# Earlier filler matmuls in any free bank, another order of loads, and the last output in three parts, in a fused RetNet and MLP kernel

## The chip, the cores and the metric

The kernel runs on one core of a Trainium2 chip. The metric is the device time of one execution in microseconds (us), the median over several runs. A core has a matrix engine (TensorE, "PE" in the profile), three engines for elementwise work (VectorE "DVE", ScalarE "ACT", GpSimd "POOL"), a queue engine that mostly issues transfers (SyncE, "SP"), and 16 DMA engines that move data between HBM and on-chip memory. Matrix products land in PSUM, which has eight banks; the other on-chip memory is SBUF.

## What is computed

The first half is a linear-attention recurrence over 4 batches, 8 heads, 768 positions and a head size of 64. Its output, 3072 tokens of 512 numbers, goes through a two-layer network with a squared ReLU.

```python
gamma = 1.0 - 2.0 ** (-5.0 - np.arange(H))
for t in range(S):
    state = gamma * state + einsum('bhd,bhe->bhde', k[:, :, t], v[:, :, t])
    y[:, :, t] = scale * einsum('bhd,bhde->bhe', q[:, :, t], state)
x = y.transpose(0, 2, 1, 3).reshape(3072, 512)
h = maximum(x @ w_in, 0)          # w_in: 512 x 2048
out = (h * h) @ w_out             # w_out: 2048 x 512
```

Inputs and output are float32; the matrix products run on bfloat16 copies.

## The kernel before, in words

**Tiling.** The 3072 tokens are cut into 24 chunks of 128. The recurrence is done chunk by chunk: inside a chunk through a masked score matrix, between chunks through a 64 x 64 state for each head. Chunks 0 and 1, and chunks 2 and 3, are handled as pairs ("pair 0" and "pair 2" below) by the functions `together` and `pair_visits`; a pair's q, k and v are loaded by one DMA each of 512 KB (L418). From chunk 4 on every chunk has its own loads of 256 KB (L588) and a "visit" on TensorE. The keys and queries are cast to bfloat16, transposed (by TensorE with an identity matrix for the early chunks, L447 and L641, by a DMA transpose for most later ones, L632) and multiplied.

**The two layers.** Chunks are gathered in blocks (`BLOCKS`, of 1, 2 or 4 chunks). `ffn1` makes the hidden layer of a block in groups, each filling one PSUM bank (matmuls on L807, ReLU on ScalarE on L812, the square on VectorE on L817). For a block of two chunks a group is 8 matmuls of 256 columns and covers 2 of the 16 slices of the hidden layer, so a block has 8 groups. `ffn2` makes the output of one chunk from 16 matmuls of 512 columns in one bank (L851), in four steps of four, one step for each piece of w_out; ScalarE copies the bank out (L859), SyncE stores it (L863). For the last chunk the output is made in two halves of 256 columns, one after the other.

**Weights.** w_in comes in six pieces: `i0` to `i3` of 512 KB each (halves of the first two quarters), `i4` and `i5` of 1 MB. w_out comes in four pieces `o0` to `o3` of 1 MB. Each lands as float32 in one of four staging buffers (`wst`) and is cast to bfloat16 in two to four steps by whichever of VectorE, ScalarE and GpSimd the plan picks (L401, L399, L403). All these loads are issued by SyncE in one queue.

**The order of the work.** Every step is an entry of a plan (`Plan.add`), with an engine or several to choose from, an expected duration, what it reads and writes, and a priority. `Plan.schedule` walks through planned time and takes always the step that can start first, ties by priority; the resulting order is fixed in the program, engine by engine. `HOME` binds single steps to an engine, `RANK` overrides a priority, `ORDER` gives the order of the first loads (letter and number: q, k, v of a chunk, `i` and `o` a piece of weights). `PACE` is the chunk from which a visit's priority competes with the two layers. Four PSUM banks (`fps`, NBANK = 4) are shared by transposes, sums and both layers; `sc` and `yy` hold the scores and outputs of the recurrence.

**Fillers.** In a span of planned time that ends at `WARM` + 1 and starts at `WARM - WARMING`, the plan counts for every TensorE step the time that TensorE would idle before it and puts in so many matmuls of 256 columns on the identity matrix (L905), each planned at `FILL` = 0.215 us. Nothing reads what they write. Before the change this span is 14.5 to 21 us, the fillers write to the last of the four banks, and that bank is kept from all other steps until 21 us.

Of the kernel before, what the change touches and what calls it, by code (L numbers as in the profile page):

```python
# [14 lines left out]
AF = mybir.ActivationFunctionType  # L15
# [3 lines left out]
class Plan:  # L19
# [48 lines left out]
    def schedule(self, nbanks, max_open):  # L68
# [17 lines left out]
                    pool[e].add(o["i"])  # L86
        if "PE" in eng_free:
            eng_free["PE"] = 0.06 * PRE
        bank_free = [0.0] * (nbanks - 1) + [WARM + 1]
        bank_of = {}  # L90
        open_groups = set()
        closed = {}
# [5 lines left out]
        while done < n:  # L98
# [25 lines left out]
            if move:  # L124
# [4 lines left out]
                while sum(x[1] for x in out_) + n_desc > self.RING:  # L129
                    t = max(t, out_.pop(0)[0])  # L130
            start[i] = t
            b = o["bank"]
            if b is not None and b[0] == "open":
                k = min((x, j) for j, x in enumerate(bank_free) if x is not None)[1]
# [4 lines left out]
            if move:  # L139
                eng_free[eng] = t + hold  # L140
                if n_desc:
                    made = max(made, t + self.GEN_LATENCY) + gen
                    ready = made + 0.15
                else:
                    ready = t + hold + 0.5
                pipe = max(max(pipe, t + self.DMA_LATENCY) + cost, ready)
                late = [y for y in (max(max(y, t + self.DMA_LATENCY) + cost, ready) for y in late) if y > pipe + 0.05]
                end[i] = max([pipe] + late) + self.LAND
                out_.append((max([pipe] + late), n_desc))
                dur = hold  # L150
            else:
                if eng == "PE":
                    o["fill"] = 0
                    if WARM - WARMING < t < WARM + 1:
                        o["fill"] = int(max(0.0, t - max(eng_free[eng], WARM - WARMING) - 0.1) / FILL)
                    issued += 2 * o["fill"]
                    before = issued
                    todo, per = 2 * o["count"], dur / max(1, 2 * o["count"])
                    now = t
                    while issued + todo > edge:  # L160
                        step = max(0, edge - issued)
                        now = max(now + step * per, next_fetched)
                        issued, todo = max(issued, edge), todo - step
                        ahead = next((y for x, y in reversed(history) if x <= edge - self.AHEAD), 0.0)
                        ahead = max(ahead, crossed)
                        crossed = now
                        edge += self.BLOCK
                        next_fetched = ahead + min(5.7, max(0.3, pipe - ahead)) + self.FETCH
                    issued += todo
                    dur = now + todo * per - t  # L170
                    history.append((issued, t + dur))
                    if any(before < x <= issued for x in range(self.BLOCK0 - self.AHEAD, issued + 1, self.BLOCK)):
                        late.append(max(pipe, t + 0.4) + 1.27)
                    o["dur"] = dur
                eng_free[eng] = t + dur
                end[i] = t + dur + o["lat"]
# [26 lines left out]
AHEAD = 4  # L203
WARM = 20.0
FILL = 0.215
WARMING = 5.5
PACE = 8
LEAD = 2
NPE = 7
NTD = 8  # L210
PRE = 0
WHALF = 2
WHALFD = (0.60, 1.47, 33, 0.6)
CVT = {'DVE': 0.69, 'POOL': 1.1}
TCAST = {'DVE': 0.43, 'ACT': 0.63, 'POOL': 0.78}
TEVAC = {'ACT': 0.6, 'DVE': 0.62}
NPAIR = 2
F2LAG = 3.0
F2WAIT = 4
CAST = {"k": {"DVE": 0.43, "ACT": 0.63, "POOL": 0.78}, "q": {"DVE": 0.43, "ACT": 0.63, "POOL": 0.78}}  # L220
WCAST = {"DVE": 0.43, "ACT": 0.63, "POOL": 0.78}
EVAC = {"ACT": 0.6, "DVE": 0.62}
WPRIO = {"in": -2.0, "out": 2.0}


HOME = {'ck5': 'ACT', 'cq5': 'ACT', 'Eq0.0': 'DVE', 'cv0.0': 'DVE', 'ck0.0': 'DVE', 'cwin5.2': 'DVE', 'cv2.1': 'POOL', 'ck2.0': 'DVE', 'cwin5.0': 'DVE', 'cwin2.0': 'POOL', 'cwout0.3': 'POOL', 'cwin1.0': 'POOL', 'ck0.1': 'DVE', 'ck2.1': 'DVE'}
RANK = {}
ORDER = (
    "q0 k0 o0 i0 v0 q2 k2 o1 v2 i1 v4 i2 k4 i3 i4 q4 i5 k5 v5 v6 o2 o3 q5 v7 k6 q6 k7 q7"
)  # L230


# [8 lines left out]
def kernel(  # L241
# [279 lines left out]
    def pair_visits(m):  # L521
# [3 lines left out]
        for b2 in range(2):  # L525
            pl.add(f"A{m}.{b2}", "PE", 0.4, [f"qkT{q0}.{x}.{b2}" for x in "kq"] + [f"qkT{q0 + c}.{x}" for c in range(2) for x in "kq"],
                   banks[b2], lambda b2=b2: pair_scores(m, b2), prio=-300 + m, lat=0.25, count=16)
            for a in range(2):
                pl.add(f"P{m}.{b2}{a}", "DVE", 0.68, (banks[b2][a], "cmask2"), (f"ptp{w}.{b2}{a}",),
                       lambda b2=b2, a=a: nc.vector.tensor_tensor(  # L530
                           out=pts2[w][:, b2, a], in0=held_by[b2][:, a, :].rearrange("s (g j t) -> s g j t", g=2, j=2),
                           in1=cmask2[:, :, None, :].to_broadcast([P, 2, 2, C]), op=ALU.mult),
                       prio=urgency(m))
        tw = [f"twin{x}{w}.{b2}" for x in "kv" for b2 in range(2)]
        for c in range(2):
            if c == 1 and i + 1 == NCH - 1:
                continue
            o1 = {}
            i0 = pl.add(f"B{m + c}", "PE", 0.3, tw, (f"gB{m + c}",),
                        lambda c=c, o1=o1: pair_sums(m, c, fps[o1["op"]["bank_index"]]), prio=-290 + m, lat=0.25,  # L540
                        count=16, bank=("open", ("B", m + c), False))
            o1["op"] = pl.ops[i0]
            twin_users.append(i0)
            j0, j1 = state(m + c, 0), state(m + c + 1, 0)
            first = i + c == 0

            def add_up(j0=j0, j1=j1, first=first, o1=o1):
                cc = fps[o1["op"]["bank_index"]][:, 0:256].rearrange("s (p t) -> s p t", p=NJ)
                if first:
                    nc.vector.tensor_copy(sts[j1][:], cc)  # L550
                else:
                    nc.vector.tensor_tensor(out=sts[j1][:], in0=cc, in1=sts[j0][:], op=ALU.add)
            pl.add(f"S{m + c}", "DVE", 0.42, (f"gB{m + c}",) if first else (f"gB{m + c}", f"S{j0}"), (f"S{j1}",), add_up,
                   prio=urgency(m) - 0.5, bank=("close", ("B", m + c)))
        for b2 in range(2):
            def values_and_state(b2=b2):
# [272 lines left out]
    def rows(m):  # L829
        return where(m)[0] * S + where(m)[1] * C  # L830

    def ffn2(blk):
        for q4 in range(blk0[blk], blk0[blk] + blocks[blk]):
            g, u = divmod(q4, 4)
            h2 = h2s[g % NH2]
            slot = q4 % NOSB
            parts = 2 if q4 == NM - 1 else 1
            w = DM // parts
            for part in range(parts):
                ns = slice(part * w, part * w + w)  # L840
                grp = ("f2", q4, part)
                keys = [f"osb{slot}.{part}"] if parts > 1 else [f"osb{slot}.0", f"osb{slot}.1"]
                o1 = {}
                for j in range(4):
                    reads = [f"h{g % NH2}.{u}.{4 * j + c}" for c in range(4)] + [f"wout{j}.{c}.{h}" for c in range(4) for h in range(2)]

                    def mm(j=j, o1=o1, h2=h2, u=u, ns=ns, w=w):
                        ps = fps[o1["op"]["bank_index"]]
                        for c in range(4):
                            fb = 4 * j + c  # L850
                            nc.tensor.matmul(ps[:, 0:w], lhsT=h2[:, fb, u * C : u * C + C], rhs=w_out_bf[j][:, c, ns],  # L851
                                             start=(fb == 0), stop=(fb == NFB - 1))
                    i0 = pl.add(f"F2.{q4}.{j}" + f"/{part}" * (parts > 1), "PE", 0.866 / parts, reads, (f"g{grp}",), mm,
                                prio=(q4 + F2LAG) * 8 + 2 * j + 1 + part * 9, lat=0.2,
                                bank=("open", grp, True) if j == 0 else ("use", grp), count=4)
                    if j == 0:
                        o1["op"] = pl.ops[i0]
                pl.add(f"O{q4}" + f"/{part}" * (parts > 1), "ACT", 0.2 + 0.4 / parts, (f"g{grp}",), keys,
                       lambda o1=o1, slot=slot, ns=ns, w=w: nc.scalar.activation(  # L859
                           osbs[slot][:, ns], fps[o1["op"]["bank_index"]][:, 0:w], AF.Copy),  # L860
                       prio=q4, bank=("close", grp))
                pl.add(f"st{q4}" + f"/{part}" * (parts > 1), "SP", STORE, keys, (),
                       lambda q4=q4, slot=slot, ns=ns: nc.sync.dma_start(out[rows(q4) : rows(q4) + C, ns], osbs[slot][:, ns]),  # L863
                       prio=-1)

    dma_prio = {x: n for n, x in enumerate(dma_order(NM))}
# [30 lines left out]
    if tc is not None:  # L897
        with tc.manual_schedule():
# [3 lines left out]
            for i in sequence:  # L902
                o = pl.ops[i]
                for _ in range(o.get("fill", 0)):
                    nc.tensor.matmul(fps[NBANK - 1][:, 0 : 2 * P], lhsT=ident[:],  # L905
                                     rhs=ident[:, None, :].to_broadcast([P, 2, P]), start=True, stop=True)
                o["fn"](o["on"]) if o["flex"] else o["fn"]()
    return pl
# [30 lines left out]
```

## Time and profile before

| what | us |
|---|---|
| median of 6 runs | 213.9 (212.88 to 214.45) |
| the profiled execution | 214.32 |
| its span in the profile | 212.6 |
| TensorE busy with matmuls | 195.7 |
| first layer's matmuls (L807), busy | 92.7 |
| second layer's matmuls (L851), busy | 89.7 |
| first matmul of any kind starts | 5.41 |
| first matmul of the first layer starts | 17.70 |
| last copy of the output ends (209.36 + 0.38) | 209.74 |

The page cuts the span in 40 slices and prints the busy tenths of each engine, so one slice is 5.3 us. "Waits" name an engine and line, what it waited for, the total in us, how often, and the longest. In the timeline a row is start, duration, engine, line, operation, output<-inputs, shapes and count; in square brackets stands how long the engine idled before, and who ended that. Matmuls of a row overlap each other, so a row's duration is from the first start to the last end.

### The profile page before, as it was taken

The page shows a single profiled execution, that of the slowest core. Times are in us where ns is not written, and L with a number is a line of the kernel's source. Part 1 is how long each engine was busy: PE and PEld are TensorE (multiplying, and loading weights), DVE is VectorE, ACT ScalarE, POOL GpSimd, SP SyncE. Part 2 cuts the span into 40 slices and gives each one's busy share as a digit, 9 for nine tenths or more (in the row PEclk, how much of TensorE's full clock was granted, in tenths as well). Part 3 has the DMA queues.
Part 4 walks back from the last instruction along what each step waited for, and adds up shares of the span by engine and source line. Part 5 has one row for each costly group of instructions (what it writes and reads, how often), then busy time and mean ns, then how long its engine had stood idle before and what let it go on. Part 6 is the DMA issues. An engine that isn't in the chain of part 4 may idle for free.

```text
span 212.6 us, 5916 instructions
## 1 busy us (share of the span) xinstructions
PE 195.7 (92%) x2545; PEld 116.9 (55%) x2570; DVE 115.0 (54%) x253; ACT 88.4 (42%) x148; POOL 42.0 (20%) x69
## 2 busy tenths in 40 slices
PE   0689799998999899999999999999999999999993
PEld 0457596773676757766654444454444444444453
DVE  3687879747385866367570765846463442322100
ACT  8335376653342434433322365223534324534221
POOL 6345333124322121312221232022000000000000
PEclk9999999999999999999999999999999999999999
DMA  6999999999899999999989997999111011011022
GB/s 164 307 301 264 328 375 315 256 310 217 226 200 179 213 208 238 241 173 200 257 176 239 246 243 146 176 228 219 25 52 52 0 52 49 0 49 51 3 99 99
DMA packets 94442, 38.13 MB, mean 179 GB/s; under 512 B 79952, under 2 KB 88400, under 8 KB 94416
## 3 DMA queue, kind: packets, MB, share of 16 engines
q1 hardware_dynamic: 94416, 37.76, 80.7%
q8 instruction: 20, 0.33, 0.7%
q14 instruction: 6, 0.05, 0.1%
HBM read 27.26 MB, written 6.29 MB: 158 GB/s over the span
## 4 chain that ended last, share of the span: by engine, by line
PE 62%; DMA 21%; SPq 11%; issue 1%; ACT 1%; DVE 1%; POOL 1%; ACTq 0%; POOLq 0%
PE fps L851 32%; PE fps L807 25%; DMA qn<-in_q_dram 7%; DMA wst<-in_moe_w_out_dram 5%; DMA kn<-in_k_dram 4%; SPq L781 4%; SPq L418 4%; DMA qkT<-kqs 3%; SPq L588 2%; DMA vn<-in_v_dram 2%; PE yy L658 2%; PE yy L673 1%; PE sc L684 1%; SPq L632 1%; PE sc L695 1%
## 5 line engine op out<-in xcount | busy, mean ns | idle before, releaser
L807 PE MATMUL fps<-xt,w_in 128*128 128x256 bf16 (+2 forms) x637 | 92.7, 294 | 1.3 <-POOL w_in L403 1.1
L851 PE MATMUL fps<-w_out,h 128*128 128x512 bf16 (+1 forms) x378 | 89.7, 370 | 2.4 <-POOL w_out L403 0.8
L812 ACT ACTIVATE h<-fps 128x512 bf16<-128x512 f32 x96 | 56.9, 596 | 76.4 <-PE fps L807 76.0
L807 PEld LDWEIGHTS <-w_in 128*128 128x128 bf16 x640 | 56.9, 98 | 32.0 <-POOL w_in L403 1.4
L817 DVE TENSOR_TENSOR h<-h 128x512 bf16<-128x512 bf16 x96 | 43.0, 458 | 48.9 <-ACT h L812 48.5
L851 PEld LDWEIGHTS <-h 128*128 128x128 bf16 x400 | 37.7, 98 | 37.5 <-issue 0.8
L859 ACT ACTIVATE osb<-fps 128x512 f32<-128x512 f32 (+1 forms) x25 | 14.5, 580 | 31.8 <-PE fps L851 31.5
L403 POOL CAST kqs<-kn 128x512 bf16<-128x512 f32 x19 | 12.6, 664 | 54.7 <-DMA kn<-in_k_dram 35.9
L760 DVE TENSOR_TENSOR xt<-yy,yf 128x512 bf16<-128x512 f32 x20 | 13.7, 686 | 16.2 <-PE yy L673 12.0
L403 POOL CAST kqs<-qn 128x512 bf16<-128x512 f32 x19 | 12.5, 656 | 19.9 <-DMA qn<-in_q_dram 18.2
L599 DVE TENSOR_TENSOR vs<-vn,vf 128x512 bf16<-128x512 f32 x20 | 13.6, 684 | 4.0 <-DMA vn<-in_v_dram 4.0
L751 DVE TENSOR_TENSOR state<-sc,state 128x256 bf16<-128x256 f32 x33 | 13.8, 419 | 0.5
L738 DVE TENSOR_TENSOR pt<-sc,cmask 128x512 bf16<-128x512 f32 x20 | 13.6, 680 | 0.0
L447 PE MATMUL fps<-ident,h 128*128 128x128 bf16 x32 | 4.6, 309 | 6.1 <-DVE h L401 6.1
L673 PE MATMUL yy<-qkT,state 64*64 64x64 bf16 x296 | 10.0, 197 | 0.2
L658 PEld LDWEIGHTS <-vs 64*64 64x64 bf16 x320 | 4.2, 107 | 6.9 <-issue 6.8
L684 PE MATMUL sc<-qkT 64*64 64x64 bf16 x320 | 6.2, 194 | 0.9 <-DMA qkT<-kqs 0.9
L399 ACT ACTIVATE qkT<-fps 128x512 bf16<-128x512 bf16 x8 | 4.7, 596 | 5.3 <-PE fps L447 4.7
L447 PEld LDWEIGHTS <-h 128*128 128x128 bf16 x32 | 3.0, 135 | 7.0 <-DVE h L401 6.4
L403 POOL CAST w_out<-wst 128x512 bf16<-128x512 f32 x5 | 4.0, 806 | 13.2 <-DMA wst<-in_moe_w_out_dram 13.2
L403 POOL CAST w_in<-wst 128x512 bf16<-128x512 f32 x6 | 4.7, 784 | 9.3 <-DMA wst<-in_moe_w_in_dram 9.3
L658 PE MATMUL yy<-pt,vs 64*64 64x64 bf16 x320 | 6.4, 198 | 0.1
(65 smaller groups left out, 88.5 us busy)
## 6 DMA issues: line engine op xcount, KB each, us to landing
out_dram<-osb SPq DMA_DIRECT2D x23, 256.0 KB, 3.8
vn<-in_v_dram SPq DMA_DIRECT2D x20, 256.0 KB, 5.0
kn<-in_k_dram SPq DMA_DIRECT2D x20, 256.0 KB, 4.9
qn<-in_q_dram SPq DMA_DIRECT2D x20, 256.0 KB, 4.7
wst<-in_moe_w_out_dram SPq DMA_DIRECT2D x4, 1024.0 KB, 9.7
wst<-in_moe_w_in_dram SPq DMA_DIRECT2D x4, 512.0 KB, 7.7
wst<-in_moe_w_in_dram SPq DMA_DIRECT2D x2, 1024.0 KB, 9.4
qn<-in_q_dram SPq DMA_DIRECT2D x2, 512.0 KB, 6.0
```

The lines of the kernel that those rows point to most:

```text
L403: nc.gpsimd.tensor_copy(o, t)
L599: lambda: nc.vector.tensor_tensor(out=o[:], in0=t.rearrange("s (h d) -> s h d", h=H), in1=vf[:, i, :, None].to_broadcast([P, H, D]), op=AL ...
L658: nc.tensor.matmul(yy[L * c : L * c + L, sub, p * L : p * L + L], lhsT=vs[r, 4 * a + j, :], rhs=pt[r, a, j, :], start=(p == 0), stop=True, ...
L673: nc.tensor.matmul(yy[L * c : L * c + L, sub, p * L : p * L + L], lhsT=st[r, j, :], rhs=qkT[r, 1, j, sub * L : sub * L + L], start=False, ...
L738: lambda: nc.vector.tensor_tensor(out=pt[:], in0=sc[:, :, 0:256].rearrange("s g (p t) -> s g p t", p=NJ), in1=cmask[:, None, None, :].to_b ...
L751: f = lambda cc=cc, j1=j1, j0=j0: nc.vector.tensor_tensor(out=sts[j1][:], in0=cc, in1=sts[j0][:], op=ALU.add)
L760: lambda: nc.vector.tensor_tensor(out=xt[:, :, u * C : u * C + C].rearrange("s p (g t) -> s g p t", g=2), in0=yy[:, :, 0:256].rearrange("s ...
L807: nc.tensor.matmul(ps[:, u * n : u * n + n], lhsT=w_in_bf[j][:, cb, c * P : (c + 1) * P], rhs=xt[:, cb, cols], start=(cb == 0), stop=(cb = ...
L812: nc.scalar.activation(h2[:, f0 : f0 + per, cols], ps[:].rearrange("p (u n) -> p u n", u=per), AF.Relu)
L817: nc.vector.tensor_mul(hv, hv, hv)
L851: nc.tensor.matmul(ps[:, 0:w], lhsT=h2[:, fb, u * C : u * C + C], rhs=w_out_bf[j][:, c, ns], start=(fb == 0), stop=(fb == NFB - 1))
L859: lambda o1=o1, slot=slot, ns=ns, w=w: nc.scalar.activation(osbs[slot][:, ns], fps[o1["op"]["bank_index"]][:, 0:w], AF.Copy),
```

## The change

The span in which fillers may be placed now starts at 1.6 us of planned time (`WARMING` 18.4) instead of 14.5. No bank is kept back for them: a filler goes to the bank that has been free longest, if there is one free at the time at which TensorE falls idle. The order of loads is new: both pairs' q, k and v and chunk 4's k come first, then w_in with chunk 4's v in between, then the first half of w_out. `PACE` goes from 8 to 6, the planned cost of GpSimd's scaling of v from 1.1 to 1.3 us, `HOME` has other entries, one of the four decay tables (`yf2`) gets a later priority, and the copy of a batch's first state may go to ScalarE. The output of the last chunk is made in three parts of 256, 128 and 128 columns, and the store of the last part is issued by ScalarE instead of SyncE. A branch for steps named in `ROUND` is added; `ROUND` is empty.

```diff
-        bank_free = [0.0] * (nbanks - 1) + [WARM + 1]
+        bank_free = [0.0] * nbanks
...
+            before_open = list(bank_free)
...
-                    if WARM - WARMING < t < WARM + 1:
+                    free = [(x, j) for j, x in enumerate(before_open) if x is not None and x <= max(eng_free[eng], WARM - WARMING)]
+                    if WARM - WARMING < t < WARM + 1 and free:
                         o["fill"] = int(max(0.0, t - max(eng_free[eng], WARM - WARMING) - 0.1) / FILL)
+                        o["fill_bank"] = min(free)[1]
...
-WARMING = 5.5
-PACE = 8
+WARMING = 18.4
+PACE = 6
...
-CVT = {'DVE': 0.69, 'POOL': 1.1}
+CVT = {'DVE': 0.69, 'POOL': 1.3}
...
+LAST = [256, 128, 128]
...
-HOME = {'ck5': 'ACT', 'cq5': 'ACT', 'Eq0.0': 'DVE', 'cv0.0': 'DVE', 'ck0.0': 'DVE', 'cwin5.2': 'DVE', 'cv2.1': 'POOL', 'ck2.0': 'DVE', 'cwin5.0': 'DVE', 'cwin2.0': 'POOL', 'cwout0.3': 'POOL', 'cwin1.0': 'POOL', 'ck0.1': 'DVE', 'ck2.1': 'DVE'}
-RANK = {}
+HOME = {'cwin5.0': 'DVE', 'cv0.1': 'DVE', 'cwin3.0': 'ACT', 'cq0.0': 'DVE', 'cwin1.0': 'DVE', 'cwin4.2': 'DVE', 'ck4': 'ACT', 'cwin5.3': 'ACT', 'cwin0.0': 'ACT', 'cwin5.1': 'ACT', 'cv0.0': 'DVE', 'cwin4.0': 'DVE', 'cq2.0': 'ACT'}
+ROUND = []
+RANK = {'yf2': -1.9}
 ORDER = (
-    "q0 k0 o0 i0 v0 q2 k2 o1 v2 i1 v4 i2 k4 i3 i4 q4 i5 k5 v5 v6 o2 o3 q5 v7 k6 q6 k7 q7"
+    "k0 q0 v0 k2 k4 q2 v2 i0 i1 i2 i3 i4 v4 i5 q4 v5 o0 o1 q5 k5 o2 k6 o3 k7 q6 v6 q7 v7"
 )
...
-            def add_up(j0=j0, j1=j1, first=first, o1=o1):
+            def add_up(on="DVE", j0=j0, j1=j1, first=first, o1=o1):
                 cc = fps[o1["op"]["bank_index"]][:, 0:256].rearrange("s (p t) -> s p t", p=NJ)
                 if first:
-                    nc.vector.tensor_copy(sts[j1][:], cc)
+                    copy_on(on, sts[j1][:], cc)
...
-            parts = 2 if q4 == NM - 1 else 1
-            w = DM // parts
-            for part in range(parts):
-                ns = slice(part * w, part * w + w)
+            widths = LAST if q4 == NM - 1 else [DM]
+            parts = len(widths)
+            for part, w in enumerate(widths):
+                lo = sum(widths[:part])
+                ns = slice(lo, lo + w)
...
-                pl.add(f"st{q4}" + f"/{part}" * (parts > 1), "SP", STORE, keys, (),
-                       lambda q4=q4, slot=slot, ns=ns: nc.sync.dma_start(out[rows(q4) : rows(q4) + C, ns], osbs[slot][:, ns]),
+                at_end = parts > 1 and part == parts - 1
+                pl.add(f"st{q4}" + f"/{part}" * (parts > 1), "ACT" if at_end else "SP", STORE, keys, (),
+                       lambda q4=q4, slot=slot, ns=ns, at_end=at_end: (nc.scalar if at_end else nc.sync).dma_start(
+                           out[rows(q4) : rows(q4) + C, ns], osbs[slot][:, ns]),
                        prio=-1)
...
-                    nc.tensor.matmul(fps[NBANK - 1][:, 0 : 2 * P], lhsT=ident[:],
+                    nc.tensor.matmul(fps[o["fill_bank"]][:, 0 : 2 * P], lhsT=ident[:],
                                      rhs=ident[:, None, :].to_broadcast([P, 2, P]), start=True, stop=True)
```

The plan's durations for the last chunk's steps follow the widths of the parts.

More of the change, by code (lines that the diff above doesn't have):

```diff
@@ L528, in pair_visits @@
             for a in range(2):
+                if f"P{m}.{b2}{a}" in ROUND:
+                    t = pts2[w][:, b2, a]
+                    pl.add(f"Pc{m}.{b2}{a}", "ACT", 0.6, (banks[b2][a],), (f"ptp{w}.{b2}{a}",),
+                           lambda b2=b2, a=a, t=t: nc.scalar.activation(
+                               t, held_by[b2][:, a, :].rearrange("s (g j t) -> s g j t", g=2, j=2), AF.Copy), prio=urgency(m))
+                    pl.add(f"Pm{m}.{b2}{a}", "POOL", 1.2, (f"ptp{w}.{b2}{a}", "cmask2"), (f"ptp{w}.{b2}{a}",),
+                           lambda t=t: nc.gpsimd.tensor_tensor(
+                               out=t, in0=t, in1=cmask2[:, :, None, :].to_broadcast([P, 2, 2, C]), op=ALU.mult),
+                           prio=urgency(m))
+                    continue
                 pl.add(f"P{m}.{b2}{a}", "DVE", 0.68, (banks[b2][a], "cmask2"), (f"ptp{w}.{b2}{a}",),
@@ L545, in pair_visits @@
             first = i + c == 0
-            def add_up(j0=j0, j1=j1, first=first, o1=o1):
+            def add_up(on="DVE", j0=j0, j1=j1, first=first, o1=o1):
                 cc = fps[o1["op"]["bank_index"]][:, 0:256].rearrange("s (p t) -> s p t", p=NJ)
                 if first:
-                    nc.vector.tensor_copy(sts[j1][:], cc)
+                    copy_on(on, sts[j1][:], cc)
                 else:
                     nc.vector.tensor_tensor(out=sts[j1][:], in0=cc, in1=sts[j0][:], op=ALU.add)
-            pl.add(f"S{m + c}", "DVE", 0.42, (f"gB{m + c}",) if first else (f"gB{m + c}", f"S{j0}"), (f"S{j1}",), add_up,
+            pl.add(f"S{m + c}", {"DVE": 0.42, "ACT": 0.45} if first else "DVE", 0.42, (f"gB{m + c}",) if first else (f"gB{m + c}", f"S{j0}"), (f"S{j1}",), add_up,
                    prio=urgency(m) - 0.5, bank=("close", ("B", m + c)))
@@ L836, in ffn2 @@
             slot = q4 % NOSB
-            parts = 2 if q4 == NM - 1 else 1
-            w = DM // parts
-            for part in range(parts):
-                ns = slice(part * w, part * w + w)
+            widths = LAST if q4 == NM - 1 else [DM]
[3 more added lines that the diff above has]
+                ns = slice(lo, lo + w)
                 grp = ("f2", q4, part)
-                keys = [f"osb{slot}.{part}"] if parts > 1 else [f"osb{slot}.0", f"osb{slot}.1"]
+                keys = [f"osb{slot}.{part}"] if parts > 1 else [f"osb{slot}.{y}" for y in range(len(LAST))]
                 o1 = {}
@@ L852, in mm @@
                                              start=(fb == 0), stop=(fb == NFB - 1))
[L853 removed]
+                    i0 = pl.add(f"F2.{q4}.{j}" + f"/{part}" * (parts > 1), "PE", 0.866 * w / DM, reads, (f"g{grp}",), mm,
                                 prio=(q4 + F2LAG) * 8 + 2 * j + 1 + part * 9, lat=0.2,
@@ L857, in ffn2 @@
                         o1["op"] = pl.ops[i0]
-                pl.add(f"O{q4}" + f"/{part}" * (parts > 1), "ACT", 0.2 + 0.4 / parts, (f"g{grp}",), keys,
+                pl.add(f"O{q4}" + f"/{part}" * (parts > 1), "ACT", 0.2 + 0.4 * w / DM, (f"g{grp}",), keys,
                        lambda o1=o1, slot=slot, ns=ns, w=w: nc.scalar.activation(
```

## The prediction

> **What bounds the kernel now.** I read the page first (busy shares, slices), then the waits of TensorE, then the timeline of the first 26 us, then the chain of waits at the end.
>
> ```profile
> span 212.6 us, 5916 instructions
> PE 195.7 (92%) x2545; PEld 116.9 (55%) x2570; DVE 115.0 (54%) x253; ACT 88.4 (42%) x148; POOL 42.0 (20%) x69
> PE   0689799998999899999999999999999999999993
> DMA  6999999999899999999989997999111011011022
> ```
>
> See two things: TensorE is full from about slice 5 on, and the DMA engines are full until slice 28, 150 us. So the end is "the moment at which TensorE has work without gaps, plus the work that is left". The gaps, from TensorE's waits:
>
> ```profile
> PE fps L447 <- DVE h L401: 6.1, 2, 5.4
> PE fps L494 <- DVE h L434: 1.2, 1, 1.2
> PE fps L807 <- POOL w_in L403: 1.1, 1, 1.1
> PE sc L684 <- DMA qkT<-kqs: 0.9, 2, 0.6
> PE fps L851 <- POOL w_out L403: 0.8, 1, 0.8
> ```
>
> After 26 us only 0.8 (at 48.5 us, for the last piece of w_out) and 0.9 are left. What the change can win lies in the first 26 us:
>
> ```profile
> 12.55 0.60 PE L447 MATMUL fps<-ident,h 128*128 128x128 bf16 x4
> 16.14 0.63 PE L905 MATMUL fps<-ident 128*128 128x256 bf16 x2
> 17.13 0.64 PE L478 MATMUL sc<-qkT 64*64 64x128 bf16 x16
> 17.70 1.35 PE L807 MATMUL fps<-xt,w_in 128*128 128x256 bf16 x8
> 18.99 0.42 PE L478 MATMUL yy<-qkT 64*64 64x128 bf16 x16
> 19.74 1.04 PE L807 MATMUL fps<-xt,w_in 128*128 128x256 bf16 x8
> 22.38 1.05 PE L807 MATMUL fps<-xt,w_in 128*128 128x256 bf16 x8
> 23.49 1.23 PE L807 MATMUL fps<-xt,w_in 128*128 128x256 bf16 x8
> 25.84 1.38 PE L807 MATMUL fps<-xt,w_in 128*128 128x256 bf16 x11 [1.12 <-POOL w_in L403]
> ```
>
> The same 16 score matmuls take 0.64 us before 18.4 us and 0.42 after: the array is at half rate until then (the trace's clock record turns to 1.0 at 18.37; the slice row prints 9 all along and does not show it). By 25.84 us four groups of the first layer are done; a group of 8 at 256 columns takes 0.87 us at full rate (the chain of waits has "0.87 PE fps L807 x8"). What held them is w_in:
>
> ```profile
> 20.00 0.63 ACT L399 ACTIVATE w_in<-wst 128x512 bf16<-128x512 f32 x1 [0.30 <-DMA wst<-in_moe_w_in_dram]
> 24.88 0.43 DVE L401 CAST w_in<-wst 128x512 bf16<-128x512 f32 x1 [0.81 <-DMA wst<-in_moe_w_in_dram]
> ```
>
> The trace's landing records give spacings of full streaming: 1.80 us per 512 KB pair load, 1.50 per half piece of weights (512 KB), 2.75 per 1 MB piece, 1.04 per 256 KB load. Streaming alone would put the fourth half piece (i3) at 22.0; it landed at 24.86. Fifteen DMA engines finished i2 by 18.45, the last at 19.98. The records of queue q8 show a 16 KB packet starting at 17.01, another at 22.35; each time the slowest engine falls back, by 1.5 and 1.3 us, and that lag of 2.85 stays through 42 us.
>
> The end:
>
> ```profile
> 207.66 0.38 ACT L859 ACTIVATE osb<-fps 128x256 f32<-128x256 f32 x1 [1.15 <-PE fps L851]
> 209.36 0.38 ACT L859 ACTIVATE osb<-fps 128x256 f32<-128x256 f32 x1 [1.31 <-PE fps L851]
> ```
>
> **What the skill says.** (1) "TensorE: Matmul & The Clock Gate", Part 1: the array starts at half clock and gets full clock after about 3.4 us of sustained activity, judged in free-running windows. The trace agrees: TensorE is busy without long gaps from 11.8 us, and the clock rises at 18.37. (2) "Runtime: NRT & Kernel Launch", Instruction fetch mechanics: instructions come in 16 KiB blocks of 256 by a DMA of the sequencer, a cost that is mostly hidden. The blocks agree (2545+2570 TensorE instructions / 256 = 20; q8 has 20 packets; 17.01 and 22.35 lie at about instruction 276 and 532), but hidden it is not: the 1.5 us above. (3) "DMA: Bandwidth & Descriptors", Issuing engines are not separate DMA queues: another issuing engine saves only sequencer time. No trace here has a store from ScalarE.
>
> **The change, part by part.**
>
> *Fillers.* They may now start from 1.6 us of the plan and use any free bank. Until the first transpose at about 5.4 us that is (5.4-1.6-0.1)/0.215 = 17 fillers, 34 instructions; perhaps 12 more in later gaps. They run where TensorE waits for data; a filler is 256 columns, 0.11 us warm (0.87/8), twice that cold, planned as 0.215, so it fits its gap. Cost on the path: 0, covered by those waits; if data comes earlier than planned, one gap's fillers, up to 0.3. A filler that waits for its bank's reader delays only the step behind it, which waits for data too. Gain: full clock by about 5.1 to 8.5 instead of 18.4. On pair 0 and pair 2 each burst gets 0.2 shorter, some six on a pair's chain, 1.2 us. This is not summed: the loads bound those pairs. It is needed, because TensorE now would idle until w_in comes.
>
> *Loads.* Streaming spacings from the first landing at 4.9: k0 4.9, q0 6.7, v0 8.5, k2 10.3, k4 11.35, q2 13.15, v2 14.95, then i0 16.45, i1 17.95, i2 19.45, i3 20.95, i4 23.7, v4 24.7, i5 27.5, q4 28.5, v5 29.5, o0 32.3, o1 35.0, q5 36.1, k5 37.1, o2 39.9, k6 40.9, o3 43.7. Instruction fetches come on top. Pair 0 has 240 TensorE instructions (16 transposes, 32 scores, 32 sums, 32 values, 8 applies, times two), with fillers the 276th falls at about 11 us, and the 532nd at the end of pair 2, about 18. I take the same 1.5 and 1.3 us: v2 16.45, i0 17.95, i1 20.8, i2 22.3, i3 23.8, i4 26.5, i5 30.3, o3 46.6. Between landing and use lie casts, 0.75 to 0.98 (i3 before: 24.86 to 25.84); I take 0.85. HOME moves casts between engines, PACE and RANK shift ties; these engines are 20 to 54% busy, and I price them at 0, with 0.3 either way.
>
> *TensorE from there.* xt of pair 0 is ready at about 13, of pair 2 at about 19. Each half piece now feeds two groups, 1.74 us. i0: 18.8 to 20.6. i1: usable 21.7 (1.1 idle), to 23.4. i2: to 25.2. i3: to 26.9. Eight groups by 26.9; before it was four by 25.84. Gain 4 x 0.87 - 1.06 = 2.4 us. After that, i4 usable at 27.4 (0.5 idle), its four groups to 30.9; i5 at 31.2 (0.3 idle), to 34.7; chunk 4's visit and first layer (3.7) fill to 39; o0 and o1 give 1.74 each (two groups may be open), to 42.6; then chunk 5 (q5, k5 by 43) to 47, with about 0.3 idle; o3 is usable at 47.5, when TensorE still has work. Idle 1.1 against 0.83 before: -0.3.
>
> *Does the lead survive?* Work that is ready but not done, the second layer above all, is smallest at about 66 us: six chunks through the first layer, about 4.4 through the second, 1.6 x 3.46 = 5 us. The lead of some 2 us is under it, so it stays. Cover gone, it costs the whole lead (rival C).
>
> *The end.* Parts of 256, 128, 128 columns: matmuls 16 x (2 x 0.056 - 0.109) = +0.06 us. The last ScalarE copy: 512 columns 0.597, 256 take 0.384, so 128 about 0.28: -0.10. The last store is 64 KB instead of 128, of 1.74 us from issue to landing (209.77 to 211.51), nearly all fixed: -0.05, with the hop from ScalarE to SyncE 0.03 less. A store from ScalarE's queue is not shown: bounds -0.2 to +0.4, taken as equal. Nothing is queued behind it. Sum -0.1.
>
> **Sum**: 2.4 - 0.3 + 0.1 = 2.2 us. The profiled execution took 214.32 (span 212.6 and 1.7 around it), giving 212.1; it lies 0.4 above the median of 213.9, so the forecast for the median is 211.7. The unknowns (lag 0 to 4.3 instead of 2.85 is about +1.5 to -1.3; casts 0.3; store 0.4; fillers 0.3) make 210.2 to 213.3.
>
> **Rivals.**
> A, the forecast, 211.7: chance 0.53.
> B, the second fetch falls on another DMA engine than the first (the fetch at 32.18 added no lag before): weights land 1.3 earlier, the 1.1 idle goes, and i4 and i5 follow: 2.2 + 1.4 = 3.6, 210.3. For: the third fetch. Against: the second did add. 0.18.
> C, the lead is given back: DMA is full until 150 us, and visits stand in a fixed place behind their transposes (0.64 us waited at 69.7). Ahead by 2 us, TensorE waits 2 us more there. 213.8. Against: the 5 us of ready work. 0.14.
> D, slower: the clock. Fillers planned at 0.215 run at 0.11 once warm, so gaps are half filled; between pair 0 and i0 (13 to 18.8) TensorE does little else. If the clock falls there and returns late, the first groups cost 1.74 each. Eight cold groups end at 18.8 + 13.9 = 32.7, 5.8 later; about 0.8 of later idle takes that to 5.0, net 2.8 slower, 216.7. It decides from the point where over 2.2 us net is lost, the clock still half at about 24 us. For: two warm-up windows are needed again. Against: with 45 to 60% busy stretches and a 1.1 us wait, the clock before did not fall at 20 to 26 us. 0.15.
>
> **How the numbers follow.** A measurement of this kernel tells 0.5%, 1.07 us, from no change. Faster: nearly all of B and 0.52 of A's 0.53, 0.70. Same: C and edges, 0.16. Slower: D less its mild half, 0.14. The range for 8 in 10 takes A and B and most of C: 209.9 to 213.9; D is left out.
>
> **What would show it.** Fillers: matmuls of 256 columns on ident from about 1.7 us, and a burst of 16 scores at 0.42 in pair 0. Loads: w_in's first cast at 17 to 18.5. Four first-layer groups more at 27 us. The wait for w_out at 48.5 gone; waits for qkT not over 2 us. The last copy under 0.3 us, the last landing about 1.7 after its issue. Wrong if w_in's groups start after 21, if bursts are 0.64 at 19 or later, or if TensorE waits for qkT or kqs between 50 and 85.

## The result

The changed kernel takes 212.68 us in the median (211.97 to 214.69) against 214.15 us before: ratio 0.9938, 95% interval 0.9924 to 0.9953, so by the ratio 1.3 us less (by the two medians 1.5). The forecast was 2.2 us less, 211.7 us, range 209.9 to 213.9. The profiled execution took 212.15 us (span 210.4) against 214.32 (212.6); this pair differs by 2.2 us, more than the medians do. Executions of one kernel lie up to 2.9 us apart (212.88 to 215.8 before), and a trace is one execution. So whether one kernel is faster than another is told here by the ratios, and the traces tell where the time goes; a small difference between two traces is trusted only where further traces repeat it. "By the ratio" always means against the kernel before.

The page after, its span, TensorE and DMA rows:

```profile
span 210.4 us, 6011 instructions
PE 198.6 (94%) x2592; PEld 119.0 (57%) x2618; DVE 112.6 (54%) x248; ACT 90.3 (43%) x153; POOL 39.9 (19%) x70
...
PE   6885999998999999999999999999999999999994
...
DMA  6999999998999999999999999899311011011022
```

TensorE is now busy from the first slice on. Its busy time rose by 2.9 us. The fillers alone take 6.8 us (34 matmuls in their group) and compute nothing that is used; all other matmuls together take less than before. The waits of TensorE after the change (engine, line, what it waited for, us in total, times, longest):

```profile
PE fps L499 <- POOL h L439: 2.4, 1, 2.4
PE fps L923 <- POOL ident L339: 1.7, 1, 1.7
PE fps L867 <- POOL w_out L408: 0.7, 1, 0.7
PE fps L867 <- issue: 0.5, 3, 0.2
```

The wait for w_in (1.1 us before) is gone, and in this execution also the waits for the transposes qkT (0.9). The wait for w_out is still there, 0.7 against 0.8. The first 26 us of TensorE, from the timeline after:

```profile
1.71 3.89 PE L923 MATMUL fps<-ident 128*128 128x256 bf16 x18 [1.71 <-POOL ident L339]
8.45 0.42 PE L483 MATMUL sc<-qkT 64*64 64x128 bf16 x16
15.09 0.42 PE L483 MATMUL sc<-qkT 64*64 64x128 bf16 x16
17.88 0.60 PE L499 MATMUL fps<-h 64*64 64x64 bf16 x32 [2.38 <-POOL h L439]
18.64 1.56 PE L822 MATMUL fps<-xt,w_in 128*128 128x256 bf16 x8
20.13 0.64 PE L509 MATMUL sc<-h,h 64*64 64x128 bf16 x16
22.13 9.89 PE L822 MATMUL fps<-xt,w_in 128*128 128x256 bf16 x88
```

Read the durations of equal bursts: 0.42 us for 16 score matmuls at 8.45, which before took 0.64 until 18.4. The array was at full clock from 5.3 us. Then it waits 2.4 us for the scaled v of pair 2, and at 18.64 a group of the first layer takes 1.56 us instead of 1.05: the clock record shows half clock from 19.0 to 22.4. From 22.13 on the first layer runs without a gap, 3.7 us earlier than the gapless stretch began before (25.84), but with one group done instead of four. The head start is thus 3.7 - 3 x 0.87 = 1.1 us, not 2.4.

And it is not what carries on behind 48 us. The stretch there, before and then after:

```profile
47.42 0.29 PE L695 MATMUL sc<-vs,kqs 64*64 64x64 bf16 x8
48.54 1.89 PE L851 MATMUL fps<-w_out,h 128*128 128x512 bf16 x7 [0.83 <-POOL w_out L403]
50.53 0.40 PE L641 MATMUL fps<-ident,kqs 128*128 128x128 bf16 x4
...
55.00 0.31 PE L684 MATMUL sc<-qkT 64*64 64x64 bf16 x16
```

```profile
45.06 0.40 PE L656 MATMUL fps<-ident,kqs 128*128 128x128 bf16 x4
...
46.15 1.06 PE L822 MATMUL fps<-xt,w_in 128*128 128x128 bf16 x16
47.88 2.75 PE L867 MATMUL fps<-w_out,h 128*128 128x512 bf16 x12 [0.67 <-POOL w_out L408]
...
53.84 0.31 PE L699 MATMUL sc<-qkT 64*64 64x64 bf16 x16
```

In both kernels TensorE runs dry and starts again when the last piece of w_out is cast. The landing records have that piece at 47.57 us before and 46.91 after, and TensorE restarts 0.66 us earlier: as much as the piece is earlier. The head start does not move that moment. From the restart to the scores (the last line of each) it takes 5.96 us instead of 6.46: chunk 6's k lands at 44.12 instead of 49.80, ahead of the piece, so that its transposition (45.06 against 50.53) is done before the wait. The end after:

```profile
207.46 0.28 ACT L875 ACTIVATE osb<-fps 128x128 f32<-128x128 f32 x1 [0.61 <-PE fps L867]
207.76 0.37 ACTq L880 DMA_DIRECT2D out_dram<-osb  x1
```

The last copy takes 0.28 instead of 0.38, and the store lands at 209.38, 1.6 us after its issue, where it was 1.74.

### The profile page after: what moved, and what is told of

Read it like the earlier page. It is cut to its first block, busy times and chain, and to the rows that moved or that the text cites. A ratio compares the mean times of both kernels' runs of the same rounds, so it can differ in the third digit from the quotient of the medians.

```text
span 210.4 us, 6011 instructions
## 1 busy us (share of the span) xinstructions
PE 198.6 (94%) x2592; PEld 119.0 (57%) x2618; DVE 112.6 (54%) x248; ACT 90.3 (43%) x153; POOL 39.9 (19%) x70
## 4 chain that ended last, share of the span: by engine, by line
PE 70%; DMA 18%; SPq 6%; POOL 1%; issue 1%; ACT 1%; DVE 1%; ACTq 0%
PE fps L867 34%; PE fps L822 30%; DMA wst<-in_moe_w_out_dram 8%; DMA wst<-in_moe_w_in_dram 5%; SPq L796 4%; DMA qn<-in_q_dram 3%; DMA vn<-in_v_dram 2%; PE yy L673 2%; PE yy L688 1%; SPq L423 1%; PE sc L710 1%; PE sc L699 1%; SPq L647 1%; DVE xt L775 1%; POOL w_out L408 1%
## 5 line engine op out<-in xcount | busy, mean ns | idle before, releaser
L867 PE MATMUL fps<-w_out,h 128*128 128x512 bf16 (+2 forms) x393 | 89.7, 362 | 2.3 <-POOL w_out L408 0.7
L832 DVE TENSOR_TENSOR h<-h 128x512 bf16<-128x512 bf16 x96 | 42.9, 454 | 51.3 <-ACT h L827 50.9
L867 PEld LDWEIGHTS <-h 128*128 128x128 bf16 x416 | 38.0, 98 | 37.3 <-issue 0.8
L875 ACT ACTIVATE osb<-fps 128x512 f32<-128x512 f32 (+2 forms) x26 | 14.7, 565 | 32.1 <-PE fps L867 32.1
L775 DVE TENSOR_TENSOR xt<-yy,yf 128x512 bf16<-128x512 f32 x20 | 13.7, 687 | 13.7 <-PE yy L688 11.8
L408 POOL CAST kqs<-kn 128x512 bf16<-128x512 f32 x19 | 12.1, 635 | 47.0 <-DMA kn<-in_k_dram 35.2
L923 PE MATMUL fps<-ident 128*128 128x256 bf16 x34 | 6.8, 347 | 1.7 <-POOL ident L339 1.7
L688 PEld LDWEIGHTS <-state 64*64 64x64 bf16 x296 | 6.1, 107 | 0.4 <-PE yy L688 0.4
L710 PE MATMUL sc<-vs,kqs 64*64 64x64 bf16 x288 | 6.2, 193 | 0.0
L923 PEld LDWEIGHTS <-ident 128*128 128x128 bf16 x34 | 3.8, 123 | 3.0 <-POOL ident L339 1.7
```

Of the source, the lines that this page charges most:

```text
L408: nc.gpsimd.tensor_copy(o, t)
L688: nc.tensor.matmul(yy[L * c : L * c + L, sub, p * L : p * L + L], lhsT=st[r, j, :], rhs=qkT[r, 1, j, sub * L : sub * L + L], start=False, ...
L775: lambda: nc.vector.tensor_tensor(out=xt[:, :, u * C : u * C + C].rearrange("s p (g t) -> s g p t", g=2), in0=yy[:, :, 0:256].rearrange("s ...
L832: nc.vector.tensor_mul(hv, hv, hv)
L875: lambda o1=o1, slot=slot, ns=ns, w=w: nc.scalar.activation(osbs[slot][:, ns], fps[o1["op"]["bank_index"]][:, 0:w], AF.Copy),
```

## The experiments

Each run was timed beside the kernel before, on the same chip. "In the same order" means that the planned order of all instructions is kept and only the named ones are added or left out.

**1. No fillers.** `a_nofill`: the changed kernel, same order.

```diff
-                for _ in range(o.get("fill", 0)):
+                for _ in range(0):
```

> The changed kernel, every instruction in the same order, without any filler. Theory 1 (the fillers carry the new load order: without them TensorE is at half clock when w_in arrives): clock full only after 20 us, first layer's groups at 1.7 us until then, 1 to 2.5 us slower than the changed kernel, ratio to the kernel before 0.998 to 1.006. Theory 2 (the load order alone brings the gain, TensorE waits for w_in anyway): as the changed kernel, 0.994. Beside that: the first instruction fetch on q8 moves from 12.8 to about 15 us, and v2 lands near 15 instead of 16.2, if the fetch is what delays it.

Measured: 0.9992 (0.9977 to 1.0007) against 0.9938, so the fillers are worth about half a per cent in the changed kernel. But the trace doesn't show it where theory 1 had it:

```profile
18.87 1.89 PE L822 MATMUL fps<-xt,w_in 128*128 128x256 bf16 x8 [1.11 <-ACT w_in L404]
20.69 0.64 PE L509 MATMUL sc<-h,h 64*64 64x128 bf16 x16
22.69 10.19 PE L822 MATMUL fps<-xt,w_in 128*128 128x256 bf16 x88
```

The clock is at half until 23.6 us, a group costs 1.89, and still the gapless stretch starts only 0.56 us later than with fillers. The instruction fetch moved from 12.8 to 14.6 us, and v2's last DMA engine finished at 15.21 instead of 16.21, while in both traces the first engine finished at 14.66 or 14.67: the fetch is what delays one engine. The delay is not gone, it falls on the next load: i0 is complete at 18.16 instead of 17.72, and i1 to i3 are 0.44 us later too. Of the 0.56 us, 0.23 lie ahead of the first group, which now waits for i0, and 0.33 in that group itself, at half clock from end to end.

**2. Fillers in the gap too.** `a_hold`: 16 more of them in the 2.4 us wait, same order.

```diff
+                if o["name"] == "B2":
+                    for _ in range(16):
+                        nc.tensor.matmul(fps[o["bank_index"]][:, 0 : 2 * P], lhsT=ident[:], ...)
```

> The changed kernel, same order, with 16 more fillers in the 2.4 us in which TensorE waits for the scaled v of pair 2 (15.5 to 17.9 us), where the plan saw no gap. Theory 1 (that gap drops the clock to half at 19.0 for 3.4 us and this costs): clock full from about 5 us on, first group 0.87 instead of 1.56 us, pair 2's last steps 1.25 instead of 2.0, together 1.4 us faster than the changed kernel, ratio to the kernel before 0.987. Theory 2 (w_in's pieces land too late for TensorE to use a full clock there): under 0.4 us faster, ratio 0.992 to 0.994.

Measured: 0.9938 (0.9913 to 0.9962), as the changed kernel: theory 2 in its number, though not by its reason. The timeline of `a_hold`:

```profile
15.39 1.92 PE L924 MATMUL fps<-ident 128*128 128x256 bf16 x16
18.29 0.59 PE L499 MATMUL fps<-h 64*64 64x64 bf16 x32 [0.98 <-POOL h L439]
19.05 1.04 PE L822 MATMUL fps<-xt,w_in 128*128 128x256 bf16 x8
...
21.37 9.78 PE L822 MATMUL fps<-xt,w_in 128*128 128x256 bf16 x88
...
44.11 1.02 PE L867 MATMUL fps<-w_out,h 128*128 128x512 bf16 x4 [0.81 <-POOL w_out L408]
...
48.05 2.75 PE L867 MATMUL fps<-w_out,h 128*128 128x512 bf16 x12 [0.70 <-POOL w_out L408]
```

The clock stays full, the group takes 1.04, and the gapless stretch starts at 21.37, 0.76 us earlier than in the changed kernel. Then 0.81 us go at a new wait for the piece of w_out that lands at 43.1, and at the last piece TensorE is where it was, 48.05 against 47.88. The gain is there and is given back.

**3. The old end.** `a_tail`:

```diff
-LAST = [256, 128, 128]
+LAST = [256, 256]
-                at_end = parts > 1 and part == parts - 1
+                at_end = False
```

> The changed kernel with the old end: two halves of 256 columns, both stored by SyncE. Theory 1: 0.15 to 0.25 us slower than the changed kernel, ratio 0.9945 to 0.995; from the last matmul to the last landing 2.2 us instead of 1.95. Theory 2 (the store from ScalarE brings more, or costs): another difference between the two in that stretch.

Measured: 0.9962 (0.9944 to 0.9979). From the last matmul's end to the end of the span it is 3.23 us (208.92 to 212.15) against 2.96 after (207.42 to 210.38): 0.27. The ratio differs by more, 0.24% or 0.5 us, but the two intervals overlap; the traces decide for the smaller. In another point this trace is worth a look. Up to the last chunk the kernel is the changed one, and yet its waits have this line:

```profile
PE sc L699 <- DMA qkT<-kqs: 0.9, 2, 0.5
```

The waits for the transposes, which the profiled execution of the changed kernel does not show, are thus not gone for good (they come at 64.3 and 87.7 us here).

**4. Fillers alone.** `b_fillf`: the kernel before in its own order, with 33 more fillers.

```diff
+                    o["more"] = o["fill"]
+                    if WARM - 18.4 < t < WARM + 1:
+                        o["more"] = int(max(0.0, t - max(eng_free[eng], WARM - 18.4) - 0.1) / FILL)
...
-                for _ in range(o.get("fill", 0)):
+                for _ in range(o.get("more", 0)):
```

> The kernel before, same order and loads, with fillers from the identity on (in the bank that it keeps free). Theory 1 (without the new load order the first layer still waits for w_in until 25.8 us): the clock is full by 9 us, bursts of the pairs are shorter, and the time is the same, ratio 0.998 to 1.001. Theory 2 (the early clock is the whole gain): 0.994.

Measured: 0.9994 (0.9966 to 1.0021), with the clock at full from 7.4 us in the profiled execution. An early clock alone brings nothing that this measurement can tell, which leaves room for 0.3%. In 10 of the 14 executions the granted clock, the mean share of full clock over an execution, was 0.976 to 0.992. In the profiled execution of the changed kernel 0.991 stands for one stretch of 3.4 us at half clock, so in these ten the clock fell again.

**5 to 8. The last piece of w_out.** From 1 to 4 followed the theory that the landing of `o3` decides. Three kernels move it (the plan then also shifts some stores and loads behind it), and a fourth takes the new end alone to the kernel before. `a_o3`, and the same with experiment 2's fillers as `a_hold_o3`:

```diff
-    "... o0 o1 q5 k5 o2 k6 o3 k7 q6 v6 q7 v7"
+    "... o0 o1 q5 k5 o2 o3 k6 k7 q6 v6 q7 v7"
```

> The changed kernel with the last piece of w_out ordered ahead of chunk 6's k, so one 256 KB load (1.04 us) earlier; the plan shifts some stores and loads behind it. Theory 1 (what TensorE did before 48 us is given back there, because everything loaded has been used up and the last piece of w_out decides): the piece lands near 45.9 instead of 46.9, the wait of 0.67 us for it at 47.9 goes to nearly 0, TensorE's visit of chunks 5 and 6 at 53.8 comes 0.5 to 0.7 earlier if chunk 6's loads allow it, ratio to the kernel before 0.990 to 0.992 against 0.9938 of the changed kernel. Theory 2 (the end is set elsewhere): no difference.

> a_hold and a_o3 together. Theory 1: the 0.8 us that the full clock gave at 21 us is no longer lost at the last piece of w_out, but the piece before it, which lands at 43.1 as it did, takes most of it; 0 to 0.6 us faster than a_o3, ratio 0.988 to 0.991. Theory 2 (head start lost for another reason): as a_hold, 0.993 to 0.994.

`a_o3late`:

```diff
-    "... o0 o1 q5 k5 o2 k6 o3 k7 q6 v6 q7 v7"
+    "... o0 o1 q5 k5 o2 k6 k7 q6 o3 v6 q7 v7"
```

> The changed kernel with the last piece of w_out ordered two loads of 256 KB later. Theory 1: it lands near 49, TensorE waits about 2.7 us for it instead of 0.67, ratio 0.999 to 1.004. Theory 2: under 0.5 us slower, ratio up to 0.996.

`b_tail`: the kernel before with the changed kernel's loop over `widths`, all else in the same order.

> The kernel before with only the new end: parts of 256, 128 and 128 columns, the last stored by ScalarE; every other instruction in the same order. Theory 1 (a shorter last copy and store): 2.0 instead of 2.2 us from the last matmul to the last landing, ratio 0.998 to 1.0. Theory 2 (more): ratio under 0.998.

Measured: `a_o3` 0.9923 (0.9905 to 0.9941), `a_o3late` 1.008 (1.0056 to 1.0105), `a_hold_o3` 0.9892 (0.9876 to 0.9907), `b_tail` 0.9993 (0.997 to 1.0017). TensorE's waits around 48 us in `a_o3`, from the timeline, and then two of the waits of `a_o3late`:

```profile
43.74 1.89 PE L867 MATMUL fps<-w_out,h 128*128 128x512 bf16 x8 [0.34 <-POOL w_out L408]
...
50.20 0.40 PE L656 MATMUL fps<-ident,kqs 128*128 128x128 bf16 x4 [0.43 <-POOL kqs L408]
...
53.58 0.31 PE L699 MATMUL sc<-qkT 64*64 64x64 bf16 x16
```

```profile
PE fps L867 <- POOL w_out L408: 3.1, 1, 3.1
...
PE sc L699 <- DMA qkT<-kqs: 1.0, 1, 1.0
```

Two loads later loses all that the change brought and more; the loss is larger than expected, because a transpose then comes late as well. One load earlier, the wait for `o3` is gone as expected (what is left, 0.34 us at 43.7, is for the piece before it). But the scores come at 53.58 instead of 53.84, 0.26 us earlier and not the expected 0.5 to 0.7: the next load binds, chunk 6's q, whose cast TensorE awaits for 0.43 us at 50.2. The ratio of `a_o3` is the expected one, but its interval overlaps that of the changed kernel, so this run alone does not show a gain. `a_hold_o3` against `a_hold` does (0.9892 against 0.9938, intervals apart). It is the fastest kernel of all, 211.43 us in the median (4 runs). Experiment 2's fillers, worth nothing alone, may bring something here; its interval and that of `a_o3` just touch. `b_tail`'s effect is not told from none; its trace has 2.94 us from the last matmul to the end, 0.29 less than before.

**9 to 11. What are the fillers worth?** The half per cent of experiment 1 didn't fit a wait for w_out. The changed kernel and the one without fillers ran again on one chip, and beside them `a_o3` without fillers.

> The changed kernel once more, beside the same kernel without fillers on one chip. Theory 1 (at 48 us the last piece of w_out decides, so the fillers alone bring little): 0 to 0.5 us faster than without fillers. Theory 2 (fillers bring about 1.1 us, as the separate comparisons suggest): 0.8 to 1.4 us faster; ratio to the kernel before near 0.994 in both.

> The changed kernel without any filler, once more. Theory 1: ratio 0.994 to 0.9965. Theory 2: 0.998 to 1.0.

> The changed kernel with the last piece of w_out one load earlier, and without any filler. Theory 1 (with that piece out of the way TensorE's own progress decides): 0.6 to 1.2 us slower than the same with fillers, ratio 0.995 to 0.999 against 0.9923, and the wait for w_out at 47 us near 0. Theory 2 (fillers are worth nothing there): 0.992 to 0.994.

Measured: `after2` 0.9955 (0.9934 to 0.9975), `a_nofill2` 0.9986 (0.9962 to 1.0011), `a_nofill_o3` 0.9917 (0.9896 to 0.9938). Two answers: the fillers bring 0.3 to 0.5% in the changed kernel (by the ratios 0.7 us in this second comparison, between the two theories of `after2`, with overlapping intervals), and nothing that can be told once `o3` is one load earlier (0.9917 without, 0.9923 with, on two chips). On one chip, without fillers, the earlier `o3` gains clearly: 0.9917 against 0.9986. Theory 1 of `a_nofill_o3` is wrong. The wait in its trace shows why:

```profile
PE fps L867 <- POOL w_out L408: 0.8, 1, 0.8
```

Even at half clock until 22.0 us TensorE reaches this point (47.5 us) before the weights do. All traces side by side, the landing of `o3` from the records of landings:

| kernel | `o3` lands | span |
|---|---|---|
| before | 47.57 | 212.6 |
| b_fillf | 48.1 | 212.7 |
| b_tail | 47.2 | 212.3 |
| after | 46.9 | 210.4 |
| after2 | 47.6 | 210.8 |
| a_hold | 47.1 | 211.1 |
| a_tail | 47.0 | 212.1 |
| a_nofill | 47.4 | 210.9 |
| a_nofill2 | 48.5 | 212.1 |
| a_nofill_o3 | 46.5 | 210.4 |
| a_hold_o3 | 46.2 | 209.6 |
| a_o3 | 45.6 | 209.8 |
| a_o3late | 50.0 | 214.0 |

Among the kernels with the new loads and the new end the span follows the landing almost one to one over 4.4 us (a straight line through the nine has a slope of 1.0, through the eight without `a_o3late` 0.8), and not the fillers: span less landing is 163.2 to 164.2 us, with or without fillers. The scatter of 1 us in that is as large as most of the differences, so a single pair can depart from it: from after to `a_o3` the landing is 1.3 us earlier, the span 0.6. And the kernels with the old loads lie beside that line, at 164.6 to 165.1, as does `a_tail` with 165.2. In the two traces without fillers and with the old place of `o3`, `o1` lands at 37.8 and 38.3 instead of 36.8 and 37.4, after instruction fetches at 34.8 and 34.1 that fall at 28.8 to 29.1 with fillers. So the fillers seem to help by moving the fetches, 34 fillers being 68 instructions, and through them the weights. That was not tried alone (fillers elsewhere, or fewer of them with more columns), and stays open. With `o3` moved, too, it lands 0.9 us later without fillers, and that trace is 0.6 us longer, which the ratios do not show.

**What of the gain is steady?** `after2` says that the landing is not the whole account of the change itself:

```profile
48.56 2.75 PE L867 MATMUL fps<-w_out,h 128*128 128x512 bf16 x12 [0.69 <-POOL w_out L408]
...
54.52 0.31 PE L699 MATMUL sc<-qkT 64*64 64x64 bf16 x16
```

Here `o3` lands and TensorE restarts when they did before (48.56 against 48.54), and still the span is 1.8 us shorter. Three traces have the old order of loads and four the new one with fillers and `o3` in its place; in stages (us):

| kernel | visit of chunks 5 and 6 starts | from there to the last matmul | waits for qkT in that | last matmul to the end |
|---|---|---|---|---|
| before | 54.53 | 154.79 | 0.91 | 3.23 |
| b_fillf | 55.22 | 154.28 | 0 | 3.25 |
| b_tail | 54.17 | 155.18 | 1.13 | 2.94 |
| after | 53.38 | 154.04 | 0 | 2.96 |
| after2 | 54.05 | 153.78 | 0 | 2.95 |
| a_tail | 53.44 | 155.47 | 0.93 | 3.23 |
| a_hold | 53.54 | 154.60 | 0.39 | 2.94 |

The visit comes 1.0 us earlier on average, and the new end saves 0.3. Together that is the 1.3 us of the ratio. Of the 1.0, half is the transposition of chunk 6's k ahead of the wait: from the restart to the visit it takes 5.49 or 5.50 us in all four new traces, 5.99 in before and `b_tail`. The other half is the landing of `o3`, on average 47.1 instead of 47.6, which the scatter (46.9 to 47.6 against 47.2 to 48.1) does not set apart; the same amount of data is loaded ahead of it in both orders. The long stretch behind the visit, its waits for qkT taken off, is not shorter with the change (153.8 to 154.5 against 153.9 to 154.3). Those waits come and go with the old loads and the new. This sum is of single executions, and no run has the transposition alone.

## Why the prediction was right, and where it was not

Direction, range and order of size were right; by the ratio the gain was 1.3 of the forecast 2.2 us. The path to it was not the forecast one, so that the number came out near is in good part luck. One of the prediction's own signs of being wrong came ("bursts are 0.64 at 19 or later": 0.64 at 20.13), and two signs of being right did not: the wait for w_out at 48 us stayed, and by 27 us about 6.4 groups of the first layer were done, not eight.

- **What bounds the kernel.** "The moment at which TensorE has work without gaps, plus the work that is left" was the wrong reading of a right observation. The moment that counts is not 26 us, where the longest gap was, but 48 us, where a gap of only 0.8 us marked that TensorE had used up everything loaded. `a_hold` shows that what TensorE gains ahead of that moment does not last; `a_o3late`, `a_hold_o3` against `a_hold`, and `a_nofill_o3` against `a_nofill2` show that the place of `o3` in the queue changes the time.
- **Fillers.** Cost 0 on the path held: the first transpose came at 5.48 instead of 5.41. The clock rose at 5.3, inside the stated 5.1 to 8.5. (The reading of the trace before was loose there: from 11.8 to 18.37 are 6.6 us, not 3.4; in the changed kernel 3.6 lie between the first filler and the rise.) That they are "needed" was wrong for the reason given: without them the gapless stretch begins 0.56 us later, and with `o3` moved no loss can be told. In the changed kernel they are worth 0.3 to 0.5% all the same, by a way that the prediction did not have.
- **Rival D, the clock falling between pair 0 and i0,** came about in mechanism in the profiled execution: half clock from 19.0 to 22.4. Keeping it at full (`a_hold`) did not change the ratio. The rival had been priced with only 0.8 us taken up by later waits; the waits for w_out at 44 and 48 us take up the whole head start of `a_hold`. That the half clock costs nothing is not shown, though: of the 37 executions of the changed kernel 13 had a granted clock of 0.983 or 0.984, and their median is 213.1 us, that of the other 24 (0.990 to 1.0) 212.6. A late load can both lengthen the gap and delay the end, so which of them is the cause stays open.
- **Loads.** Lag 1.5 us from a fetch at about 11 us: the fetch came at 12.8, and v2 landed at 16.21 (forecast 16.45), i0 at 17.72 (17.95). The second fetch came at 21.9, not 18, so i1 to i3 landed 1.6 earlier than forecast. `o3` was forecast at 46.6 and landed at 46.91, which is partly luck: with the forecast lag of 2.85 us `o0` and `o1` would have landed at 35.15 and 37.85, and they landed 1.2 and 1.1 us earlier. Rival B, weights landing about 1.3 us earlier than in A, thus happened for w_in, and brought nothing that lasted: the idle of 1.1 us at i1 did not occur because TensorE was the later one.
- **"Eight groups by 26.9"**: about 6.4 by the count of columns. The plan puts the last steps of pair 2 between the first and the second group, and they and the first group ran at half clock.
- **"Does the lead survive?" is the step that failed.** It looked for the smallest store of ready work at 66 us and found 5 us (its own product, 1.6 x 3.46, is 5.5). At 48 us the store was empty. The error came a line earlier: "then chunk 5 (q5, k5 by 43) to 47". A visit of TensorE takes the values of one chunk and the scores of the next in one step, `visit(m, n)`, so chunk 5's output, and with it its first layer, waits for chunk 6's loads, which are complete at 50.8 after and 50.9 before. In both kernels this visit comes at 53 to 55 us (the score bursts above), and the 3.7 us of work that were to bridge the time until `o3` came after it.
- **Rival C, the lead given back,** is what happened to the 1.1 us, but at w_out and not, as the rival had it, at the transposes. In the two profiled executions the last matmul ends 1.9 us earlier: the restart at `o3` comes 0.66 earlier, the transposition ahead of the wait gives 0.5, so that the scores at 55.00 come at 53.84, and the two waits for qkT of 0.64 and 0.27 us are not there (other small gaps take 0.16 of them back), because chunk 9's transpose, for one, lands at 67.7 instead of 69.6. The last term is of these two executions and not of the change: `a_tail` waits 0.9 us for qkT again, `a_hold` 0.4.
- **The end**: forecast 0.1 us, measured 0.27. The copy gained 0.10 as stated, the store 0.12 instead of 0.05, and 0.05 lie behind its landing; the matmuls' extra (16 x 0.003 is 0.05, not 0.06) is in the 1.9 already. The store from ScalarE cost nothing that shows: it lands 1.6 us after its issue, and so does the store of equal size that SyncE issued just before it. The forecast gain of 0.03 by the shorter hop did not come: 0.03 us lie between copy and issue in both cases.

So the profiled pair's 2.2 us equals the forecast by luck, as a sum of other terms: 0.66 from the earlier restart at 48 us, 0.5 from the transposition ahead of it, some 0.75 from the stretch behind, where this execution missed the waits for qkT, 0.27 from the end, and none of the 2.4 that were to come from TensorE's head start at w_in.

## What to carry to other kernels

Where transfers are full for most of a kernel, look for the last place at which the busiest engine runs dry. In this kernel a head start ahead of it was worth nothing that could be told, and over 4.4 us each microsecond by which the awaited piece landed earlier was worth about one, until the next load was the one awaited. A short wait (0.8 us here) can be that place, and the test is cheap: move the awaited load one place earlier and one or two later. When a trace pair differs by more than the medians, compare further traces stage by stage before a wait that is gone is put down to the change. Before counting work as "ready", look which steps the program ties together.

## What was not expected of the hardware

- One 16 KB instruction fetch put one of 16 DMA engines behind: v2's last engine finished 1.55 us after its first with the fetch at 12.8 (the last but one 0.44 after it), 0.54 us after it with the fetch at 14.6. The lag was still there in the loads behind it: 1.6 us from the first engine to the last for i0 to i3. By `o0`, at 34 us, it was 0.6.
- The clock dropped at 19.0 us after a gap of only 2.4 us, and it did not drop in `after2`, where TensorE waited 2.8 us for the same v. In the four traces with a drop the changes of clock lie a multiple of 3.41 us apart (5.34, 18.99 and 22.41 in after; 4.70, 18.35 and 21.76 in `a_tail`). Counted on in such steps, nearly all of the gap in after (15.5 to 17.9) lies in the step from 15.6 to 19.0, and that of `a_tail` (15.5 to 18.4) in the one from 14.9 to 18.4; in `after2`, where the clock rose at 6.61, a step ends at 16.9, amid the gap (15.7 to 18.5). So where the gap falls among the steps seems to decide.
- In `a_o3` the clock was at half from 13.0 to 16.4 us, with no gap over 0.4 us between TensorE's first matmul and 13.0. No run here explains it.
